# A retention layer and two expert layers on one core: the second expert layer begun on two turned tiles, and turns of the first put in front of a loop

## The chip, the core and the metric

The kernel runs on one core of one Trainium2 chip. The metric is the device time of one execution in microseconds (us). The core's engines are TensorE (PE; PEld is its weight loading), VectorE (DVE), ScalarE (ACT), GpSimd (POOL) and SyncE (SP, which only issues DMAs). Each engine takes its instructions in the order in which the program gives them; engines meet through semaphores.

## The reference

```python
def _attn_ref(q, k, v):                      # 8 batches, 8 heads, 576 positions, 64 dims
    scores = scale * np.matmul(q, k.transpose(0, 1, 3, 2))
    ret = scores * Dmat[None]                # gamma_h ** (i - j) for i >= j, else 0
    return np.matmul(ret, v)

def _moe_ref(x, w_skip, w_gate, w1, w2):     # 4608 tokens of 512, 8 experts, 1024 hidden
    do_compute = x @ w_skip > 0
    xc = x[do_compute]
    e_idx, gate_w = ...                      # largest logit of xc @ w_gate, and its probability
    for e in range(8):
        y[e_idx == e] = gate_w * (relu(xc @ w1[e]) @ w2[e])
    out[do_compute] = xc + y

def _moe2_ref(x, w_gate, w1, w2):
    # (token, expert) pairs in falling order of their logit; each token goes to the first expert
    # that still has room, each expert takes at most 576 tokens
    for e in range(8):
        out[assigned == e] = relu(x[assigned == e] @ w1[e]) @ w2[e]
```

The attention's output is the input of the first expert block, whose output is the input of the second.

## The kernel before, in words

The attention with its gate logits runs first, tile by tile, and ends with a routing step that gives each token of the first block its expert and its place (`route`). Then come the two expert blocks. The program's order is written out by hand: each engine executes in the order in which these Python lines issue instructions.

**An expert in either block.** Its tokens' rows are gathered from DRAM into tiles of up to 128 rows by GpSimd (`gather`, line 619), turned by four transposes on TensorE, copied out by ScalarE as the high part `xTH`, and VectorE subtracts to get the low part `xTL` (`turn`, 634: the products are made in three passes, high with high, high with low, low with high). Weights come as quarters of 512 KB (`w_load`, 229), are split into a high part by ScalarE (`w_split`, 237) and a low one by VectorE (`w_rest`, 251). Layer 1 (`layer1`, 675; `layer1_f`, 652) goes over eight filters of 128 hidden units, 12 matmuls each for a segment of columns; ScalarE and VectorE write the hidden units' high and low parts. Filters 0 and 1 need weight quarter 0, filters 2 and 3 quarter 1, and so on. Layer 2 (`layer2`, 694) multiplies these by w2, and the rows are scattered to DRAM. The first block takes at most 352 tokens of an expert in its regular pass (tiles of 128, 128 and 96); tokens beyond that go through a loop of overflow blocks (`over_blocks`, 897), whose count is computed on the chip (`nov`, 878). In this input it is zero, and the body is not run. The loop's entry and exit stay: every engine loads the count (line 899), and all engines meet before the program goes on. In the kernel before, the loop stands directly behind the issue of the three gathers of expert 0; then come filler matmuls (`warm`, 221, which keep TensorE busy and whose result nobody reads) and the three turns (1051 to 1054). The gates' weights (`gate_parts`, 808; `gate_weights`, 825) are computed in steps within layer 1 of expert 0, as jobs of `slot_a`.

**The second block.** Which tokens an expert takes depends on the experts before it, so the assignment is found in eight phases (`phase`, 1159), one per expert. A phase builds masked logits and claims (1169 to 1176), finds a threshold in five rounds (1180 to 1203; each round is a mask on VectorE, ten small matmuls `cnt`, an intermediate copy `part`, four matmuls `sum`, a comparison `fl`, one matmul `nfl`, and a maximum), gives the expert's number (`eix`, from there on its weights can be loaded), then the list of its tokens (`ids2`, from there on its rows can be gathered), and last updates the state: what room and which tokens are left (1289 to 1319). Phase 0 runs beside the first block's last layer 2, each later phase beside the layers of the expert before it.

Phases and preparations are Python generators. `tick` (1349), called twice in each filter's 12 matmuls and once per filter of layer 2, advances a clock by columns/2400 and lets every task whose time has come issue its next step between the matmuls; the number that a step yields is the time until the next. `LAG` (1165) is added to the waits in which an answer of another engine is expected.

Between the two blocks the order is written out (1376 to 1395): when list 0 is there, two weight quarters are loaded on SyncE's queue and the five tiles gathered, 64 fillers are issued, and then steps of the phases (`go`), weight splits (`sp`), turns and loads on ScalarE's queue alternate as line 1387 lists them. Five `go` are among them: two finish phase 0's state update, three begin the claims of phase 1. Four of the five turns stand in front of layer 1, the fifth is a task of its own. `eil` is a copy of expert 0's number, from which SyncE and ScalarE load the address of its weights. Layer 1 takes two segments, columns 0 to 256 (tiles 0 and 1) and 256 to 576 (tiles 2 to 4), for two filters at a time with expert 0:

```python
1463        hh = layer1(("b", i), [(0, 256), (256, CAP2)], lambda: None, 1 if i else 2, tick, ht=ht)
```

`weights_b` (1411) splits what is left of w1 (`held`, 1409), splits w2, waits for the next expert's number and loads its first quarter; `rows_b` (1445) waits for the next list, gathers its tiles, and turns them once layer 1 is done.

## Time and profile before

| | us |
|---|---|
| median of 3 runs | 971.97 |
| lowest and highest run | 970.97, 974.04 |
| the profiled execution, its own time | 971.05 |
| its span, first to last instruction | 969.3 |
| attention and routing | 0 to about 176 |
| first block, layer 1 of expert 0 to the last layer 2 | 190.4 to 478.9 |
| second block, layer 1 of expert 0 to the end | 493.1 to 969.3 |

The span is what the profile's rows cover; the time around it is 1.75 us. In the rows, times are us from the span's start unless marked ns; a name like `xTL<-trp,xTH` says what is written and what is read; the number in brackets at a row's end is how long the engine stood idle before it, and what ended that. The ends of matmuls are modelled. The granted clock is a share of TensorE's 2.4 GHz: 1.00 or 0.50.

### The profile page before, as it was taken

The numbers are of one execution on the slowest core, as the hardware profiler recorded it, in microseconds if no ns is written. First come the engines' busy times: TensorE is split into PE (matmuls) and PEld (weight loads), VectorE is DVE, ScalarE is ACT, GpSimd is POOL, SyncE is SP. The second block draws the span as 40 slices with busy tenths as digits, with TensorE's granted clock in tenths as the row PEclk, the third lists the DMA queues.
The fourth block names the chain that finished last, engine by engine and source line by source line (L and its number), as shares of the span: only waits on it lengthen the run. The fifth ranks groups of instructions, "written<-read, shape, count | busy, mean of one in ns | idle before, by whom it ended". The sixth has DMA issues, their size and how long they took to land.

```text
span 969.3 us, 20752 instructions
## 1 busy us (share of the span) xinstructions
PE 918.6 (95%) x8356; PEld 768.9 (79%) x8356; DVE 653.6 (67%) x1677; ACT 320.2 (33%) x610; POOL 232.6 (24%) x208
## 2 busy tenths in 40 slices
PE   7899998599999999998969999999999999999997
PEld 7777886498888888886658697887978879797885
DVE  3556576369999999966677767676775767844230
ACT  1233333233434333352042242332423324243330
POOL 2322231203354344231310302104031030320101
PEclk9999999799999999999989999999999999999999
DMA  9999995264454455340160515215061231533201
GB/s 318 356 377 358 347 368 228 79 234 174 159 196 138 160 181 175 133 135 11 40 222 24 205 45 192 80 51 190 34 218 55 101 139 55 207 114 115 87 6 44
DMA packets 57684, 153.96 MB, mean 159 GB/s; under 512 B 8464, under 2 KB 9232, under 8 KB 57328
## 3 DMA queue, kind: packets, MB, share of 16 engines
q1 hardware_dynamic: 40608, 107.50, 31.6%
q0 software_dynamic: 10496, 30.93, 9.1%
q10 hardware_dynamic: 6480, 14.16, 3.9%
q8 instruction: 67, 1.10, 0.5%
q14 instruction: 33, 0.27, 0.1%
HBM read 127.43 MB, written 25.13 MB: 157 GB/s over the span
## 4 chain that ended last, share of the span: by engine, by line
PE 72%; DVE 15%; DMA 7%; issue 3%; ACT 1%; SPq 1%; POOL 1%; POOLq 0%; ACTq 0%; DVEq 0%
PE l1p L660 27%; PE l2p L691 26%; DVE junk L758 5%; PE xTp L445 3%; PE trp L641 3%; PE l2p L714 2%; PE sc L419 2%; DVE w2L L179 2%; DMA vR<-in_v_r_dram 2%; DMA xg<-X,ids 2%; PE xrp L473 1%; DVE xTL L179 1%; DMA kT<-in_k_c_dram 1%; DVE hL L188 1%; PE xTp L442 1%
## 5 line engine op out<-in xcount | busy, mean ns | idle before, releaser
L660 PE MATMUL l1p<-xTH,w1H 128*128 128x320 f32 (+2 forms) x768 | 241.4, 314 | 4.9 <-DVE hL L188 3.0
L660 PE MATMUL l1p<-xTL,w1H 128*128 128x320 f32 (+2 forms) x768 | 234.2, 305 | 2.9 <-DVE xTL L179 2.9
L660 PE MATMUL l1p<-xTH,w1L 128*128 128x320 f32 (+2 forms) x768 | 233.7, 304 | 0.0
L691 PE MATMUL l2p<-w2H,hH 128*128 128x512 f32 (+1 forms) x448 | 187.9, 419 | 0.0
L691 PE MATMUL l2p<-w2H,hL 128*128 128x512 f32 (+1 forms) x448 | 177.2, 396 | 0.0
L691 PE MATMUL l2p<-w2L,hH 128*128 128x512 f32 (+1 forms) x448 | 177.0, 395 | 0.0
L660 PEld LDWEIGHTS l1p<-xTH,w1H 128*128 128x128 f32 x768 | 145.1, 189 | 9.4 <-DVE hL L188 5.6
L660 PEld LDWEIGHTS l1p<-xTL,w1H 128*128 128x128 f32 x768 | 145.1, 189 | 4.2 <-DVE xTL L179 3.8
L660 PEld LDWEIGHTS l1p<-xTH,w1L 128*128 128x128 f32 x768 | 144.9, 189 | 0.0
L188 DVE SCALAR_TENSOR_TENSOR hL<-l1p,hH 128x256 fp32r<-128x256 f32 (+1 forms) x192 | 85.6, 453 | 80.6 <-ACT hH L669 77.1
L720 POOL DMA_INDIRECT out_dram<-y,ids x40 | 41.6, 1040 | 375.9 <-DVE y L179 224.5
L669 ACT ACTIVATE hH<-l1p 128x256 fp32r<-128x256 f32 (+1 forms) x192 | 78.3, 408 | 147.7 <-PE l1p L660 141.1
L691 PEld LDWEIGHTS l2p<-w2H,hH 128*128 128x128 f32 (+1 forms) x448 | 82.9, 185 | 24.7 <-issue 8.3
L758 DVE SCALAR_TENSOR_TENSOR junk<-x,wgb 128x512 f32<-128x512 f32 (+1 forms) x144 | 99.0, 687 | 3.1
L691 PEld LDWEIGHTS l2p<-w2H,hL 128*128 128x128 f32 (+1 forms) x448 | 82.6, 184 | 22.0
L691 PEld LDWEIGHTS l2p<-w2L,hH 128*128 128x128 f32 (+1 forms) x448 | 83.1, 185 | 15.6
L621 POOL DMA_INDIRECT xg<-X,ids x64 | 78.4, 1225 | 55.2 <-issue 25.9
L245 ACT ACTIVATE w1H<-wraw 128x1024 fp32r<-128x1024 f32 x64 | 65.3, 1053 | 41.0 <-DMA wraw<-in_w1b_dram 37.9
L642 ACT ACTIVATE xTH<-trp 128x512 fp32r<-128x512 f32 (+2 forms) x64 | 35.4, 557 | 124.5 <-PE trp L641 113.5
L179 DVE TENSOR_TENSOR w2L<-wraw,w2H 128x1024 fp32r<-128x1024 f32 x60 | 72.7, 1214 | 0.0
L245 ACT ACTIVATE w2H<-wraw 128x1024 fp32r<-128x1024 f32 x64 | 67.4, 1055 | 15.4 <-PE l2p L691 7.3
L179 DVE TENSOR_TENSOR w1L<-wraw,w1H 128x1024 fp32r<-128x1024 f32 x60 | 71.5, 1216 | 0.4
(258 smaller groups left out, 1136.6 us busy)
## 6 DMA issues: line engine op xcount, KB each, us to landing
wraw<-in_w2a_dram SPq DMA_DIRECT2D x31, 512.0 KB
wraw<-in_w1b_dram SPq DMA_DIRECT2D x30, 512.0 KB
wraw<-in_w2b_dram SPq DMA_DIRECT2D x30, 512.0 KB
wraw<-in_w1a_dram SPq DMA_DIRECT2D x28, 512.0 KB
kT<-in_k_c_dram SPq DMA_DIRECT2D x36, 256.0 KB
qT<-in_q_c_dram SPq DMA_DIRECT2D x36, 256.0 KB
vR<-in_v_r_dram SPq DMA_DIRECT2D x36, 256.0 KB
X<-xo ACTq DMA_DIRECT2D x36, 256.0 KB
```

Of the source, the lines that this page charges most:

```text
L179: V.tensor_tensor(o, x, y, op)
L188: V.scalar_tensor_tensor(o, x, sc, y, op0, op1)
L245: nc.scalar.activation(h, r, AF.Copy)
L445: nc.tensor.matmul(xTp[o, hh, x:x + P], lhsT=d["vs"][:, 2 * pr + hh, :], rhs=d["ret"][:, hh, pr, :], start=(c == 0), stop=True, skip_group ...
L621: nc.gpsimd.indirect_dma_start(out=t[0:n, :], out_offset=None, in_=X[:, :], in_offset=bass.IndirectOffsetOnAxis(ap=ids[0:n, :], axis=0))
L641: nc.tensor.transpose(p[:, k, 0:n], g[0:n, k * P:(k + 1) * P], ident[0:n, 0:n])
L642: nc.scalar.activation(h[:, :, off:off + n], p[:, :, 0:n], AF.Copy)
L660: nc.tensor.matmul(o, lhsT=wx[:, c:c + P], rhs=xx[:, k, a:b], start=(n == 0), stop=(n == 11))
L669: nc.scalar.activation(hh[0][:, f, a:b], o, AF.Relu)
L691: nc.tensor.matmul(p[0:n, :], lhsT=x[:, f, off:off + n], rhs=y[:, c:c + 512], start=(f == 0 and j == 0), stop=(f == 7 and j == 2))
L720: nc.gpsimd.indirect_dma_start(out=dst[:, :], out_offset=bass.IndirectOffsetOnAxis(ap=idx, axis=0), in_=src[0:n, :], in_offset=None)
L758: V.scalar_tensor_tensor(j[0:n], x2[0:n], 1.0, wgb[e // 4][0:n, e % 4], ALU.mult, ALU.mult, accum_out=dst[0:n, e:e + 1])
```

## The change

In front of the first block, the gate parts are computed ahead, the first two tiles are turned, then comes the overflow loop, two of the three gate multiplications, and the third turn; the fillers there are dropped. Within the loop, tiles get other places in memory. In the second block, the gathers are issued first; the first step of the state update (which now includes the copy `eil`) comes ahead of SyncE's two weight loads, the second ahead of the fillers, of which 48 are left. Two tiles are turned and two weight quarters split; then layer 1 begins, four filters at a time. The three other turns and the remainder of quarter 1 are steps of a task, `entry`; the phases go on 3.5 clock units later, the splits of quarters 2 and 3 after 5. ScalarE's queue issues its loads behind the second split instead of between the turns, and the last w2 quarter waits in `held`. The lag is 0.25 instead of 0.4 in phase 1, and 0.9 instead of 1.0 from phase 2 on.

```diff
@@ -632,7 +632,10 @@
     xT = {}
 
     def turn(key, i, n, off, spare=False):
-        if i == 0:
+        if key == "o":
+            xo = xp.tile([P, 2, 4, P], F32R, name="xTo", tag="hL")
+            xT[key] = (xo[:, 0], xo[:, 1])
+        elif i == 0:
             xT[key] = (xp.tile([P, 4, CAP2], F32R, name="xTH", tag="xTH"), xp.tile([P, 4, CAP2], F32R, name="xTL", tag="xTL"))
         h, l = xT[key]
         g = xg[key, i]
@@ -806,7 +809,6 @@
 
 
     def gate_parts():
-        gs.clear()
         ex = rt("c1", [P, NC, E])[:, 0:NT]
         tt(ex, LG[:, :, 0:8], last(m1, E), ALU.subtract)
         nc.scalar.activation(ex, ex, AF.Exp)
@@ -820,12 +822,10 @@
             V.tensor_copy(gj, gw)
             tt(gw, gw, gj, ALU.subtract)
             gs.append(gj)
-            yield
 
     def gate_weights():
-        for j, _ in enumerate(gate_parts()):
-            if j:
-                tt(MV[:, :, 24 + 24 * j:48 + 24 * j], OHhi, pairs(gs[j - 1], 24), ALU.mult)
+        for j in range(3):
+            tt(MV[:, :, 48 + 24 * j:72 + 24 * j], OHhi, pairs(gs[j], 24), ALU.mult)
             yield
         gp = psm.tile([P, 72], F32, name="gp", tag="sm")
         for t in range(NT):
@@ -898,18 +898,15 @@
         kept = dict(wt)
         with tc.For_i(0, nc.values_load(nov[0:1, 0:1], min_val=0, max_val=NT + E), 1):
             over_lists()
-            for _ in gate_parts():
-                pass
             om = rt("om", [P, NT])
             ts(om, ohi, blk, ALU.is_equal)
-            MO = xp.tile([P, NT, 6], BF16, name="MO", tag="hL")
+            MO = xp.tile([P, NT, P + 6], BF16, name="MO", tag="hH")
             for j, c in enumerate((u_t, v_t, gs[0], gs[1], gs[2], oex)):
-                tt(MO[:, :, j], om, c, ALU.mult)
-            OHo = xp.tile([P, NT, P], BF16, name="OHo", tag="hH")
-            tt(OHo, mid(iota, NT), last(olo, P), ALU.is_equal)
+                tt(MO[:, :, P + j], om, c, ALU.mult)
+            tt(MO[:, :, 0:P], mid(iota, NT), last(olo, P), ALU.is_equal)
             p = psm.tile([P, 6], F32, name="ovp", tag="sm")
             for t in range(NT):
-                nc.tensor.matmul(p, lhsT=OHo[:, t, :], rhs=MO[:, t, :], start=(t == 0), stop=(t == NT - 1))
+                nc.tensor.matmul(p, lhsT=MO[:, t, 0:P], rhs=MO[:, t, P:P + 6], start=(t == 0), stop=(t == NT - 1))
             ov6 = rt("ov6", [P, 6])
             V.tensor_copy(ov6, p)
             oxi = rt("oxi", [P, 1], I32)
@@ -1046,12 +1043,17 @@
 
 
     over()
-    over_blocks()
+    gps = gate_parts()
+    next(gps)
+    next(gps, None)
     gws = gate_weights()
     t0 = turns(0, T1, (2,))
-    for n, j in enumerate(t0):
-        warm(ps1, "l1", 16 if n == 0 else 4)
-        j()
+    t0[0]()
+    t0[1]()
+    over_blocks()
+    next(gws)
+    next(gws)
+    t0[2]()
     for j in gathers_a(1):
         j()
     pend = []
@@ -1091,7 +1093,7 @@
         ga, (la1, la2) = gathers_a(e + 1), loads_a(e + 1)
         if e == 0:
             sta = state()
-            jobs += [j for n in range(4) for j in (lambda: next(gws, None), la1[n])] + [lambda: next(gws, None)]
+            jobs += [la1[0], lambda: next(gws), la1[1], lambda: next(gws, None)] + la1[2:4]
         else:
             jobs = jobs[0:2] + [ga[0]] + jobs[2:4] + [ga[1]] + jobs[4:5] + [ga[2]] + la1
         hh = layer1(e, [(0, CAP1)], slot_a)
@@ -1162,7 +1164,7 @@
         sb = rt("sb", [P, 2, NC], BF16)
         mc = rt("mc", [P, 1])
         es = rt("es", [P, E])
-        LAG = (0.3, 0.4, 1.0)[min(i, 2)]
+        LAG = (0.3, 0.25, 0.9)[min(i, 2)]
         MASK = 1.6
         if i < E - 1:
             if i:
@@ -1282,8 +1284,6 @@
                                  start=(q == 0), stop=(q == 3), tile_position=(0, 32 * a), skip_group_check=True)
         iv = rt("iv", [P, 5])
         ts(iv, p[:, 5:10], -1.0, ALU.add)
-        if i == 0:
-            V.tensor_copy(eil, eix[:, 0:1])
         stt(ids2[:, i, :], p[:, 0:5], 64.0, iv, ALU.mult, ALU.add)
         yield "list"
         if i < E - 1:
@@ -1295,6 +1295,8 @@
             ts(cnd, inv0, 1.0 / ZMUL, ALU.mult)
             V.reciprocal(cnd, cnd)
             ts(zu, zu, cnd, ALU.mult, lo0, ALU.add)
+            if i == 0:
+                V.tensor_copy(eil, eix[:, 0:1])
             X2 = rt("X2", [P, NC, E], BF16)
             tt(X2, OH[:, 0:NC], last(gh, E), ALU.mult)
             cc = rt("cc", [P, E])
@@ -1376,23 +1378,35 @@
     tasks.remove(t)
     while 0 not in listed:
         next(gen)
+    for j in gathers_b(0):
+        j()
+    go = lambda: next(gen)
+    go()
     lb = load_b(0)
-    sp = halves("w1", swap=True)
-    for j in lb[0][0:2] + gathers_b(0):
+    lb[0][0]()
+    lb[0][1]()
+    go()
+    warm(ps1, "l1", 48)
+    t0 = turns(("b", 0), T2, (2, 3))
+    t0[0]()
+    w_split("w1", 0, "later", swap=True)
+    w_rest("w1", 0)
+    t0[1]()
+    w_split("w1", 1, "later", swap=True)
+    la = load_b(0, nc.scalar)
+    for j in la[0][2:4] + la[1][0:1]:
         j()
-    t0 = turns(("b", 0), T2, (2, 3))
-    warm(ps1, "l1", 64)
-    go = lambda: next(gen)
-    la = load_b(0, nc.scalar)
-    for j in [go, go, sp[0], t0[0], sp[1], go, t0[1], go] + la[0][2:4] + [t0[2], go, t0[3], la[1][0], la[1][1]] + sp[2:5] + lb[1][2:4]:
-        j()
-
-    def last_turn():
-        t0[4]()
-        yield 0
-
-    task(last_turn())
-    task(gen)
+
+    def entry():
+        w_rest("w1", 1)
+        for j in t0[2:5]:
+            yield 0.7
+            j()
+        for j in la[1][1:3]:
+            j()
+
+    task(entry())
+    task(gen)[1] = clock[0] + 3.5
 
     def post_b(i):
         def post(j, n, p):
@@ -1406,10 +1420,12 @@
     lay = [0]
     done = set()
 
-    held = []
+    held = [lb[1][3]]
 
     def weights_b(i):
         if held:
+            if i == 0:
+                yield 5.0
             for c in (2, 3):
                 w_split("w1", c, "later", swap=True)
                 yield 1.2
@@ -1460,7 +1476,7 @@
     for i in range(E):
         mine = [task(weights_b(i)), task(rows_b(i))]
         ht = xp.tile([P, 8, 64], F32, name="hT", tag="junk", bufs=1)
-        hh = layer1(("b", i), [(0, 256), (256, CAP2)], lambda: None, 1 if i else 2, tick, ht=ht)
+        hh = layer1(("b", i), [(0, 256), (256, CAP2)], lambda: None, 1 if i else 4, tick, ht=ht)
         lay[0] += 1
         whole = [wt["whole", "w2", c] for c in range(4)]
         layer2_half(ht, whole, post_b(i), 4, tick)
```

## Rows read from the trace of the kernel before

**Rows 1.** TensorE's waits, 481 to 530 us: in total, times, longest.

```profile
PE trp L641 <- DMA xg<-X,ids: 3.9, 1, 3.9
PE l1p L660 <- DVE xTL L179: 2.4, 2, 1.4
...
PE cnt L1191 <- DVE M L179: 0.9, 1, 0.9
```

**Rows 2.** TensorE's waits, 530 us to the last layer.

```profile
PE idp L1272 <- DVE OHl L179: 1.8, 3, 0.9
```

**Rows 3.** Layer-1 matmuls by stretch: us, PE, PEld, clock, DMA.

```profile
493.06:530.02 36.96, 31.23 (x192) 27.55 (x192) 0.95 0.28 99
562.72:590.45 27.73, 27.41 (x192) 25.62 (x192) 1.00 0.13 48
911.43:936.88 25.45, 25.44 (x192) 25.17 (x191) 1.00 0.09 32
```

**Rows 4.** Chain of waits at the overflow loop: start us, us, what.

```profile
177.47 0.97 POOL xg L621
...
178.74 4.65 DMA xg<-X,ids
183.39 1.58 issue
...
190.98 1.07 PE l1p L660 x5
```

**Rows 5.** Line 899 on VectorE's sequencer: ns min/median/max, first and last start.

```profile
L899 DVEq EVENT_SEMAPHORE  x13: 21/50/3641, 179.1 to 184.4; - x13
...
L899 DVEq TENSOR_LOAD <-nov x1: 662/662/662, 178.2 to 178.2; - x1
```

**Rows 6.** Chain of waits, 482 to 504 us.

```profile
483.57 5.88 DMA xg<-X,ids
...
489.49 1.14 PE trp L641 x4
...
490.65 0.61 ACT xTH L642
...
491.97 1.13 DVE w1L L179
...
493.78 0.60 DVE xTL L179
```

**Rows 7.** VectorE by line, 196 to 205 us: busy us, mean ns.

```profile
L179 DVE TENSOR_TENSOR MV<-OHhi,gw 128x864 bf16<-128x864 bf16 x3 | 1.8, 601 | 0.0
```

**Rows 8.** Stretches at the low clock: us, five engines, clock, DMA.

```profile
179.16:189.40 10.24, 4.42 (x34) 4.31 (x35) 0.69 (x1) 0.96 (x2) 3.35 (x4) 0.50 0.39 113
...
503.43:506.84 3.41, 3.41 (x19) 3.19 (x16) 2.28 (x6) 1.44 (x3) 0.00 (x0) 0.50 0.04 18
```

**Rows 9.** DMA queues, 484.5 to 487 us: packets, MB, share.

```profile
q1 hardware_dynamic: 241, 0.92, 96.1%
```

**Rows 10.** VectorE in order of time: start us, us.

```profile
487.86 0.16 DVE L179 TENSOR_TENSOR rem<-rem,cct 128x8 f32<-128x8 f32 x1 [3.31 <-remote]
...
497.30 3.48 DVE L179 TENSOR_TENSOR w1L<-wraw,w1H 128x1024 fp32r<-128x1024 f32 x3
...
539.74 0.16 DVE L188 SCALAR_TENSOR_TENSOR ids<-idq,iv 128x5 int32<-128x5 f32 x1
```

**Rows 11.** TensorE in order of time.

```profile
481.80 3.75 PE L224 MATMUL idle<-ones 128*128 128x128 bf16 x64
...
494.43 0.38 PE L660 MATMUL l1p<-xTL,w1H 128*128 128x256 f32 x1 [0.95 <-DVE xTL L179]
...
556.74 0.46 PE L641 MATMUL trp<-cs,xg 64*128 64x64 f32 x4
```

**Rows 12.** ScalarE in order of time.

```profile
491.14 1.05 ACT L245 ACTIVATE w1H<-wraw 128x1024 fp32r<-128x1024 f32 x1
```

**Rows 13.** VectorE's busy time, 491.28 us to the layer's end.

```profile
491.28:530.02 38.74, 31.47 (x85) 0.93 0.28 96
```

## The prediction, made before the changed kernel ran

> **What bounds the kernel now.** I began with the clock line and the waits of TensorE, to find where the engine that carries the kernel stands still. From 530 us to the end it waits 1.8 us for VectorE [rows 2]; an edit behind that point has little to win. Between 481 and 530 us it stands 3.9 us for the first gathered tile of the second block, 2.4 us for the low parts of the turned tiles and 0.9 us for a mask of the claims [rows 1]. The table of the layer-1 matmuls shows the same from another side [rows 3]: the same 192 matmuls take 36.96 us for the second block's first expert, 27.73 us for its second, and 25.45 us for the last, which has no claims beside it. So some 9 us are lost in that layer. The other serial place is the loop over overflow blocks in front of the first block, whose body does not run here. Its chain [rows 4] goes from the gathers to the last landing at 183.39, then 1.58 us of restart; layer 1 flows from 190.98. The loop makes every engine wait until gathers still under way have landed.
>
> **Part 1: turns and gate parts in front of the loop.** The second gather is issued at 177.47; with the 4.65 us that the third took [rows 4] it lands at 182.1. Four transposes cost 1.14 us at the low clock, the copy 0.61, the low part 0.60 [rows 6]: TensorE is done at 183.3, ScalarE at 183.9, VectorE at 184.5. VectorE loaded the loop's count at 178.2 and had waited 3.64 us when the barrier opened [rows 5], so it reached it at 183.39 - 3.64 = 179.75, 1.55 us after the load. That load now follows the second tile's low part: begun between 183.9 and 184.5, the barrier opens at 185.5 to 186.1, no longer held by the third gather (183.39). With 1.58 us of restart TensorE is back at 187.3. The third tile has 96 rows of 128: three quarters of 1.14 and 0.61 give 188.6 and its low part, about 0.5, 189.1. The two gate multiplications now in front of that low part, 0.60 us each [rows 7], run from 187.3 to 188.5, beside the transposes and the copy; without this cover they would cost 1.2 us. The rest of the gate parts runs while VectorE waits for the gathers. **Gain 190.98 - 189.1 = 1.9 us.** Moving the gates' 36 small matmuls from the end of layer 1 into its middle changes no amount of work, and the gathers of expert 1, about 2 us later, are wanted only in layer 2: nothing.
>
> Against it stands the clock. It was at 1.2 GHz, half, from 179.16 to 189.40 [rows 8]; 24 filler matmuls and three turns ran from 184.97 on, and layer 1 began at 2.4 GHz. The fillers are gone, and TensorE does two short turns, stands some 4 us and then starts on real work, so the low stretch probably lasts into layer 1. Another low stretch lasted 3.41 us [rows 8]; at half speed it costs half, 1.7 us. Bounds 0 and 1.7; I take 1.2, nearer to the upper, as less work than before precedes the layer. Part 1 nets **0.7 us** (0.2 to 1.9). "TensorE: Matmul & The Clock Gate" of the Trainium skill (Part 1, the HAM clock gate) says the throttled state is the default and activity releases it, which speaks against taking fillers out; the row agrees.
>
> **Part 2: when layer 1 of the second block starts.** Now the first gather goes out at 483.57 and lands 5.88 us later; its turn starts at 489.49 [rows 6]. The third gather of part 1 needed 4.65 us [rows 4]. The difference is the weight loads: from 484.5 to 487 us all 241 packets are theirs, on SyncE's queue, and none are the gather's [rows 9]. The change copies the expert's number six short VectorE instructions later and so issues the loads behind the gather. Landing between 488.2 (483.57 + 4.65) and 489.4; I take 488.7, since the loads still come before the later gathers. The small product of the state update, which now precedes the fillers, costs TensorE nothing measurable; before, VectorE waited 3.31 us behind 64 of them, until 487.86 [rows 10], although their own rows end after 3.75 us [rows 11]. So 48 fillers take between 2.8 us (3.75 x 48/64) and 4.5 us (487.86 - 481.80, for 64, in proportion), from 484.55 (487.86 - 3.31, when VectorE had its operand ready): done at 487.4 to 489.1, inside the same bounds. The rest of the state update, 487.86 to 491 before, then runs inside the gather's wait.
>
> From its turn to the first steady matmul took 494.43 - 489.49 = 4.94 us [rows 6, 11]. Out goes the third step of the claims between a weight remainder and the second tile's low part (491.97 + 1.13 = 493.10 to 493.78, 0.68 us [rows 6]). In comes the split of the first weight quarter, 1.05 us on ScalarE [rows 12], which now stands behind the first tile's copy (before it ran while the gather was awaited); its remainder starts after 0.61 + 1.05 instead of 0.61 + 0.69: 0.4 us. So layer 1 flows from 488.7 + 4.94 - 0.68 + 0.4 = **493.4** (492.9 to 494.2) against 494.43.
>
> "DMA: Bandwidth & Descriptors" of the Trainium skill (Queues, rings and completion order) says each DMA engine serves its queues in turn, packet by packet. By that rule the gather would have shared the engines from the start, which rows 9 do not show, and moving the loads would win nothing.
>
> **Part 3: length of that layer.** The matmuls alone take 25.45 us; five rounds of claims add 27.73 - 25.45 = 2.3 [rows 3]; three turns now stand inside the layer, each half of 1.14 at the full clock, 1.7 together. The waits behind late low parts [rows 1] go: four filters over two tiles' 256 columns come first, and the third to fifth turn have over 5 us.
>
> What is late next is VectorE. It has 31.47 us of work from 491.28 to the end of the layer [rows 13], and every answer of a claims round queues behind whatever stands ahead: a weight remainder is 3.48/3 = 1.16 us [rows 10]. The later start (3.5 units of 2,400 columns) puts the first mask at the tenth tick, beside the remainder of quarter 2, and the shorter lag (0.25 for 0.4) asks for each answer after about one tick, 0.64 or 0.8 units. Laid out tick by tick, with each engine in order, TensorE waits 0.4 us for the first mask, 0.85 for its sum, 0.15 in the second round, 0.7 in the third and 0.3 in the last: 2.4 us. Bounds: 0 (before, one wait of 0.9 us for a mask was all that the claims cost it [rows 1]) and five remainders, 5.8. Clock: the layer begins after broken work, as before at 503.43, so 0 to 1.7 again; I take 1.0. The layer ends at 493.4 + 25.45 + 2.3 + 1.7 + 2.4 + 1.0 = 526.25 instead of 530.02. **Gain 3.8 us** (from 492.9 + 29.25 = 522.1, 7.9 better, to 494.2 + 29.45 + 5.8 + 1.7 = 531.2, 1.1 worse).
>
> Behind it I count nothing: layer 2 keeps its waits for the list's one-hots (1.8 [rows 2], could go or grow by as much), the lag of 0.9 instead of 1.0 has as little cover to lose, and the quarters 2 and 3 and the fourth w2 quarter are issued later but have the layer's first half. The overflow loop's new tiles are not reached.
>
> **The rivals.** *Loads and gathers share:* part 2 wins nothing (494.2), the rest holds: 967.6. *VectorE keeps up:* no waits in part 3, clock high at once: 971.05 - 7.9 - 0.7 = 962.5; for it speaks that the same rounds cost one wait of 0.9 us before, against it that the same work of VectorE now has some 5 us less. *Nothing comes of it:* the early start is not one, since the first turn and the split queue on ScalarE, both low stretches last 1.7 us and waits reach 4.5: part 1 gives 0.2, the layer ends at 494.2 + 29.45 + 4.5 + 1.7 = 529.85: 970.7. *Slower:* the list of expert 1 comes late. It stood at 539.74 [rows 10], 9.7 us behind the layer; its fifth turn ended at 557.2 [rows 11], 5.5 us ahead of the next layer at 562.72 [rows 3]. Those 5.5 us are the point: if rounds that start later and queue behind remainders push the list further than that behind the layer's end, each further us is paid in full. With the layer 1.1 us worse, as at its upper bound, and 2.5 us paid: 974.7 in the profile, 975.6 on the runs' scale.
>
> **How the numbers follow.** 971.05 - 0.7 - 3.8 = 966.55 for the profiled execution, which lies 0.9 below the median of 971.97; I give **967.0**, between that and 967.5. A difference below 0.3% (2.9 us) cannot be told from none. Chances: forecast 0.47, sharing 0.13, keeping up 0.12 (these three faster: 0.70, as a 0.02 of the forecast's tail falls short), nothing 0.23, slower 0.05. The range, 963.2 to 970.8, takes in the first, second and most of the fourth, and leaves out the best end and the slower case.
>
> **What would show it.** Right: the barrier opens near 186 us; a low clock reaches into layer 1 of the first block; the first turn of the second block starts before 489; three turns lie among the first four filters; first steady layer 1 under 34 us, with small waits for VectorE's masks and sums. Wrong: the first turn at 489.5 or later (loads not the cause), a first layer above 35 us (VectorE's queue), or a wait of TensorE for gathered tiles ahead of the next layer (the list).

## The result: slower, and where the profile after shows it

The changed kernel takes **979.54 us** (median of 8 runs, 976.56 to 982.49) against 973.1 us of the kernel before in the same comparison: ratio **1.0071 [1.0048, 1.0095]**. Forecast were 967.0 us and a gain. The profiled execution after took 979.02 us, its span is 977.2 us (before 971.05 and 969.3).

Up to the second block's second expert the changed kernel is ahead, though less by the change than the absolute times suggest. TensorE's rows at the start of the second block, after (start us, us, what; idle before it and what ended that):

```profile
488.91 0.95 PE L644 MATMUL trp<-cs,xg 128*128 128x128 f32 x4
490.65 0.66 PE L644 MATMUL trp<-cs,xg 128*128 128x128 f32 x4 [0.79 <-DMA xg<-X,ids]
492.23 0.39 PE L663 MATMUL l1p<-xTH,w1H 128*128 128x256 f32 x1 [0.92 <-ACT xTH L645]
493.61 0.58 PE L663 MATMUL l1p<-xTL,w1H 128*128 128x256 f32 x1 [0.99 <-DVE xTL L179]
```

The first turn no longer waits for its gather, and steady work starts at 493.61 (494.43 in [rows 11]). But this execution was 0.8 us ahead before any changed line: the last matmul into `qc`, a product of the routing, stands at

```profile
170.35 0.21 PE L319 MATMUL qc<-OHe,ones 128*128 128x80 bf16 x1 [0.90 <-DVE base L185]
```
```profile
169.54 0.21 PE L319 MATMUL qc<-OHe,ones 128*128 128x80 bf16 x1 [0.91 <-DVE base L185]
```

before and after. From there to the end of the first block both executions take 308.5 us, and from that end to steady layer 1 both take 15.5 us. So the 0.8 us are not the change's. The gather did come sooner (first packet 1.7 us after its issue, 3.6 before); yet the fillers behind it now ran at the low clock, 48 of them in 5.28 us where 64 had taken 3.75 [rows 11], and TensorE left them for the first turn only at 488.91:

```profile
483.84 5.28 PE L224 MATMUL idle<-ones 128*128 128x128 bf16 x48
```

The layer-1 matmuls of the second block's first, second and last expert, after, by stretch (us, PE, PEld, clock, DMA), answer to [rows 3]:

```profile
492.23:527.12 34.89, 30.64 (x192) 27.06 (x192) 0.95 0.26 92
558.51:586.76 28.25, 27.73 (x192) 25.70 (x191) 1.00 0.14 48
919.23:944.77 25.54, 25.54 (x192) 25.27 (x191) 1.00 0.09 32
```

The first is 2.1 us shorter, and the second starts at 558.51 instead of 562.72: **4.2 us ahead**. Of these, 0.8 us are the earlier start above, 2.1 us the shorter layer, and 1.3 us lie behind it: there two waits for `OHl` cost 1.5 us before (536 to 538 us), and TensorE waits for nothing after (527.2 to 558.5). By the end the kernel is 7.9 us behind, so 12.1 us go in a stretch for which the prediction had nothing. TensorE's waits from 530 us on, after, answer to [rows 2], where `OHl` stands with three waits; the only other wait there was 0.4 us for a gathered tile:

```profile
PE trp L644 <- DMA xg<-X,ids: 5.1, 3, 2.0
PE l1p L663 <- DVE hL L188: 0.8, 1, 0.8
PE idp L1274 <- DVE OHl L179: 0.8, 1, 0.8
PE cnt L1193 <- DVE M L179: 0.7, 2, 0.4
```

TensorE now stands for gathered tiles far behind the block's start. One such place, around the list of expert 3: VectorE's list, GpSimd's gathers, SyncE's weight loads (`x3` groups three issues), and TensorE's wait.

```profile
650.31 0.17 DVE L188 SCALAR_TENSOR_TENSOR ids<-idq,iv 128x5 int32<-128x5 f32 x1
```
```profile
651.25 1.31 POOL L621 DMA_INDIRECT xg<-X,ids  x1 [30.76 <-PE l2p L717]
...
657.86 0.92 POOL L621 DMA_INDIRECT xg<-X,ids  x1 [0.30 <-issue]
```
```profile
647.52 2.32 SPq L234 DMA_DIRECT2D wraw<-in_w1b_dram  x3
651.05 8.92 SPq L234 DMA_DIRECT2D wraw<-in_w2b_dram  x3
```
```profile
658.98 0.66 PE L644 MATMUL trp<-cs,xg 128*128 128x128 f32 x4 [2.04 <-DMA xg<-X,ids]
```

The gathers go out among the loads. In the kernel before, the loads of this expert began at 651.15 and the first gather followed 6 us behind:

```profile
651.15 1.59 SPq L234 DMA_DIRECT2D wraw<-in_w1b_dram  x3
```
```profile
657.37 1.32 POOL L621 DMA_INDIRECT xg<-X,ids  x1 [1.58 <-issue]
```

The DMA queues after, from 651.5 to 655 us (packets, MB, share):

```profile
q1 hardware_dynamic: 301, 1.08, 89.3%
```

All packets but one are of the weights' queue; of the gather issued at 651.25 none moves in these 3.5 us, as in [rows 9]. What holds them back the traces do not say. Once packets of both queues move, they share the engines, as before from 657.5 to 661 us:

```profile
q1 hardware_dynamic: 276, 0.97, 69.6%
q0 software_dynamic: 109, 0.35, 26.6%
```

The turn, however, is placed by the planner's clock and comes whether or not the tile has landed. Right behind this wait TensorE drops to the low clock once more (three low stretches after: us, five engines, clock, DMA; the first answers to [rows 8], the second covers the fillers):

```profile
179.01:192.66 13.65, 8.47 (x29) 7.01 (x30) 4.98 (x14) 2.15 (x4) 3.21 (x3) 0.50 0.38 127
482.80:489.62 6.82, 5.83 (x53) 5.78 (x53) 3.24 (x17) 0.00 (x0) 4.74 (x5) 0.50 0.74 255
660.29:663.70 3.41, 3.41 (x12) 2.72 (x11) 3.23 (x8) 0.47 (x1) 1.22 (x1) 0.50 0.73 256
```

What moved the list? Reading each list's time against the end of its block's layer 1 gives the theory. The lists of experts 1 to 6 come behind the end of the layer before by (us; each the start of `ids` less the last layer-1 matmul):

| kernel | 1 | 2 | 3 | 4 | 5 | 6 |
|---|---|---|---|---|---|---|
| before | 9.7 | 7.3 | 7.3 | 7.7 | 7.2 | 7.2 |
| after | 11.3 | 7.5 | 4.2 | 0.5 | -3.1 | -5.7 |

Before, a phase lasts as long as a pair of layers and the list keeps its place. After, it walks forward by some 3.5 us per expert; this is called the drift below. The lag is not only a cover for single answers: 19 yields of a phase carry it (three in each of five rounds and four more), so 0.9 instead of 1.0 makes the phase 1.9 planner units shorter.

The drift is already in the program. A step is issued at the first tick at or after its time, ticks lie 0.64 to 0.85 units apart, and the next time counts from at most 0.4 units before that tick. Worked through with these rules and the yields of the two kernels, the lists of experts 2 to 6 stand 5.33 units behind the layer, each of them, before, and 5.33, 2.56, 0.0, -2.88 and -5.12 units after. The plain sum of a phase's yields does not show this: it is 42.7 units with the lag of 1.0 and 40.8 with 0.9, against 46.9 that a pair of layers ticks. With 1.0 the whole difference goes into waiting for ticks.

### The profile page after: what moved, and what is told of

It is laid out like the page before. It is cut to its first block, busy times and chain, and to the rows that moved or that the text cites. A ratio compares the mean times of both kernels' runs of the same rounds, so it can differ in the third digit from the quotient of the medians.

```text
span 977.2 us, 20671 instructions
## 1 busy us (share of the span) xinstructions
PE 923.8 (95%) x8316; PEld 769.5 (79%) x8316; DVE 652.0 (67%) x1677; ACT 319.3 (33%) x610; POOL 226.3 (23%) x208
## 4 chain that ended last, share of the span: by engine, by line
PE 56%; DVE 18%; issue 3%; DMA 2%; ACT 1%; another core or an unknown queue 0%; POOLq 0%; ACTq 0%; DVEq 0%
PE l2p L694 24%; PE l1p L663 23%; DVE junk L761 5%; DVE w2L L179 3%; PE l2p L717 3%; PE trp L644 2%; DVE hL L188 2%; DVE w1L L179 2%; DMA xg<-X,ids 1%; DVE xTL L179 1%; DVE x L188 1%; PE cnt L1193 1%; PE idp L1274 1%; DVE M L179 1%; PE idle L224 1%
## 5 line engine op out<-in xcount | busy, mean ns | idle before, releaser
L663 PEld LDWEIGHTS l1p<-xTH,w1H 128*128 128x128 f32 x768 | 145.7, 190 | 10.5 <-DVE hL L188 6.4
L621 POOL DMA_INDIRECT xg<-X,ids x64 | 74.2, 1160 | 163.5 <-PE l1p L663 51.4
L723 POOL DMA_INDIRECT out_dram<-y,ids x40 | 38.7, 967 | 284.9 <-ACT y L1414 121.7
L179 DVE TENSOR_TENSOR ret<-sc,cs 128x512 f32<-128x512 f32 x72 | 46.3, 685 | 33.5 <-PE sc L419 33.5
```

Of the source, the lines that this page charges most:

```text
L179: V.tensor_tensor(o, x, y, op)
L621: nc.gpsimd.indirect_dma_start(out=t[0:n, :], out_offset=None, in_=X[:, :], in_offset=bass.IndirectOffsetOnAxis(ap=ids[0:n, :], axis=0))
L663: nc.tensor.matmul(o, lhsT=wx[:, c:c + P], rhs=xx[:, k, a:b], start=(n == 0), stop=(n == 11))
L723: nc.gpsimd.indirect_dma_start(out=dst[:, :], out_offset=bass.IndirectOffsetOnAxis(ap=idx, axis=0), in_=src[0:n, :], in_offset=None)
```

## The experiments

Every run stands beside the kernel before on the same chip. From each profiled execution I also took three stretches: A from the first matmul into `qc` (line 319) to the end of the first block, B to the start of layer 1 of the second block's second expert, C to the last matmul's end. A also holds some 32 us of routing that no edit touches and that differs by up to 2 us from one execution to the next.

| kernel | median us | ratio to before | A | B | C |
|---|---|---|---|---|---|
| before | 971.2 to 973.1 | 1 | 340.8 | 83.8 | 400.3 |
| after | 979.54 | 1.0071 [1.0048, 1.0095] | 341.4 | 80.4 | 412.4 |
| after_lag10 | 970.91 | 0.9991 [0.9965, 1.0017] | 340.3 | 80.1 | 405.4 |
| before_lag09 | 978.50 | 1.0068 [1.0037, 1.0098] | 341.9 | 85.0 | 409.1 |
| before_part1 | 974.07 | 1.0029 [1.0005, 1.0053] | 341.2 | 85.2 | 401.9 |
| after_no_part1 | 979.12 | 1.0066 [1.0033, 1.0098] | 339.9 | 80.4 | 410.4 |
| lag09_once | 971.66 | 0.9995 [0.9966, 1.0023] | 341.5 | 80.7 | 403.5 |
| lag09_pad | 970.18 | 0.9960 [0.9938, 0.9981] | 342.0 | 82.0 | 401.1 |
| lag09_hold | 974.69 | 1.0010 [0.9987, 1.0034] | 340.2 | 81.7 | 406.7 |
| lag09_once_no_part1 | 971.35 | 0.9983 [0.9960, 1.0006] | 339.1 | 82.0 | 404.6 |
| lag10_drift | 980.16 | 1.0084 [1.0057, 1.0111] | 341.2 | 80.1 | 414.3 |
| before_lag09_pad | 975.38 | 1.0044 [1.0011, 1.0077] | 338.8 | 82.2 | 404.9 |
| pad_again | 969.84 | 0.9982 [0.9955, 1.0009] | 341.3 | 80.3 | 401.7 |
| pad_no_part1 | 967.98 | 0.9962 [0.9936, 0.9988] | 339.7 | 80.2 | 400.9 |
| pad_fill84 | 974.10 | 1.0033 [1.0007, 1.0058] | 343.8 | 82.0 | 401.3 |
| pad_fill20 | 971.19 | 0.9987 [0.9957, 1.0016] | 339.8 | 80.5 | 403.8 |
| best_again | 970.74 | 0.9984 [0.9951, 1.0018] | 339.5 | 81.8 | 400.6 |

**The lag, in both kernels.**

```diff
-        LAG = (0.3, 0.25, 0.9)[min(i, 2)]
+        LAG = (0.3, 0.25, 1.0)[min(i, 2)]
```

> The changed kernel with one number put back: the lag of phases 2 and later is 1.0 again, not 0.9. Theory (the lag): the shorter lag brings the lists forward against the layers, so that gathers queue among the weight loads and the turned tiles come late; that is where the 12 us behind the second block's first layer went. Then this kernel keeps the 4 to 5 us gained ahead of that layer and loses nothing behind it: 967 to 970 us, the stretch from layer 1 of the second expert to the end at 406 to 409 us, list 3 some 7 us behind the layer's end and not 4. Rival (the offset): the lists' place is set by the start of the phases 3.5 later and by phase 1's lag of 0.25, and the lag behind them matters little: 977 to 981 us, waits for gathered tiles near 659 and 776 as in the changed kernel.

And in the kernel before:

```diff
-        LAG = (0.3, 0.4, 1.0)[min(i, 2)]
+        LAG = (0.3, 0.4, 0.9)[min(i, 2)]
```

> The kernel before with the lag of phases 2 and later at 0.9 and nothing else. Theory (the lag): the lists come earlier here too and collide with the weight loads: 976 to 986 us, with TensorE waiting for gathered tiles behind 560 us. Rival (the offset): without the shifted start the shorter lag only moves small operations about: 971 to 975 us. Second rival (the sum of both): a loss of less than half of the changed kernel's 12 us, 974 to 978 us, as the lists begin from a later place than in the changed kernel.

Measured: 970.91 and 978.50. The one number brings the changed kernel 8.6 us back (7.8 by the ratios) and costs the kernel before 7 us; the rival by the offset falls in both. But 970.91 misses the theory's 967 to 970. Stretch C is 405.4 and not 400.3. The lists now hold their place, but at 10.2 to 11.9 us behind the layer, 3 us later than before. TensorE's waits from 560 us on in after_lag10 show what this place costs:

```profile
PE idp L1274 <- DVE OHl L179: 4.0, 5, 1.0
```

Once per phase the product over the list's one-hots is asked for before VectorE has written them; between 560 us and the end the kernel before has one such wait, of 0.3 us. With the lists drifting in before_lag09 the gathered tiles are late again:

```profile
PE trp L641 <- DMA xg<-X,ids: 4.1, 4, 1.8
PE idp L1272 <- DVE OHl L179: 2.4, 4, 1.0
```

**The two halves of the change.** before_part1 is the kernel before with the first block's hunks of the diff (lines 632 to 1093), after_no_part1 has all the others.

> The kernel before with the first block's half of the change alone: the first tiles turned and two of the gate's parts made in front of the loop, the loop's matrices in one tile. The second block is as before. Theory (the trace of the changed kernel: all layers of the first block 1.0 us earlier): 971.5 to 973 us, ratio 0.998 to 1.000. Rival (this part has a share of the loss, by what it does to the lists of the second block): above 975 us.

> The changed kernel without the first block's half: turns and gate parts stay in the loop's wake, the second block is as changed. Theory (all of the loss is of the second block): 979.5 to 981.5 us, about 1 us over the changed kernel, with the waits for gathered tiles behind 640 us. Rival (the two halves meet): at or under 976 us.

Measured: 974.07, where 971.5 to 973 was expected, and 979.12, just under the 979.5 to 981.5 expected. The loss belongs to the second block. The first half, however, does not gain.

**Drift or cover?** A shorter lag does two things: it shortens the phase, and it leaves VectorE less time ahead of each small matmul. Two kernels keep the short lag and take the drift away, by one short phase only (lag09_once) or by a longer last yield (lag09_pad):

```diff
-        LAG = (0.3, 0.25, 0.9)[min(i, 2)]
+        LAG = (0.3, 0.25, 0.9, 1.0)[min(i, 3)]
```

> The changed kernel with the lag of 0.9 in phase 2 alone and 1.0 from phase 3 on. Theory (place and drift): 0.9 makes a phase some 2.7 us shorter than a pair of layers, so that each list comes about 3.5 us earlier against its layer than the one before it (11.3, 7.5, 4.2, 0.5, -3.1, -5.7 us behind the end of layer 1), while 1.0 holds the place; with 1.0 throughout the lists stand 10.3 us behind the layer and each phase's matmuls with the list's digits wait 0.6 to 1.1 us for VectorE (4.0 us in all), at the 7.2 us of the kernel before they do not. So with one short phase the lists stand near 7.5 us throughout: 965.5 to 968.5 us, no wait of TensorE behind 560 us over 1 us in total. Rival (the lag itself: a shorter lag is a shorter cover wherever it stands): as with 1.0 throughout less one phase's change, 970 to 973 us. Rival (the gain ahead of the second expert cannot be kept): 970 to 972 us with 406 us turned into 410 us behind layer 1 of the second expert by waits that are new.

```diff
             tt(asg, asg, t2, ALU.add)
-            yield 1.5
+            yield 3.4 if i > 1 else 1.5
```

> The changed kernel, lag 0.9 kept in all phases from 2 on, and the last yield of those phases longer by 1.9 (19 lags of 0.1 less in each), so that a phase has its old length. Theory (drift): the lists stand 7 to 8 us behind the layer's end throughout and the loss goes: 965.5 to 969 us, no wait for gathered tiles behind 560 us. Rival (cover: 0.1 us less between VectorE's work and the small matmuls that read it is what costs): the drift is gone but each phase still waits: 975 to 980 us, with TensorE waiting for VectorE's tiles in every phase.

One makes the opposite: the long lag with a phase as short as the changed kernel's.

```diff
-        LAG = (0.3, 0.25, 0.9)[min(i, 2)]
+        LAG = (0.3, 0.25, 1.0)[min(i, 2)]
...
-            yield 2.0 + LAG
+            yield (1.3 if i > 1 else 2.0) + LAG
...
-            yield 1.5
+            yield 0.3 if i > 1 else 1.5
```

> The changed kernel with the lag at 1.0 from phase 2 on, but those phases shortened elsewhere by the same 1.9 us: 0.7 off the yield ahead of the counts' matmul and 1.2 off the last yield. Every other matmul of a phase has its old lag; the phase is as short as with 0.9. Theory (drift): the lists run forward against the layers as in the changed kernel (7, 4, 0.5, -3 us behind layer 1's end), TensorE waits for gathered tiles: 976 to 981 us. Rival (the lag of 0.9 itself costs by lost cover): no more than the run with 1.0 and nothing shortened, 970 to 973 us.

| kernel | list 1 | 2 | 3 | 4 | 5 | 6 |
|---|---|---|---|---|---|---|
| after_lag10 | 11.3 | 10.5 | 10.3 | 11.9 | 10.2 | 10.3 |
| lag09_once | 11.3 | 7.3 | 7.3 | 7.3 | 6.4 | 7.3 |
| lag09_pad | 11.3 | 7.3 | 7.3 | 7.3 | 6.4 | 7.3 |
| lag10_drift | 11.3 | 10.4 | 7.2 | 4.2 | -0.8 | -4.1 |
| before_lag09 | 10.9 | 6.6 | 3.1 | -0.8 | -4.0 | -6.4 |

Measured: lag09_pad 970.18, lag10_drift 980.16. With the short lag everywhere and no drift the loss is gone, though 970.18 lies 1.2 us above the range expected (the rival by lost cover had 975 to 980); with the long lag and the drift it is there in full. TensorE's waits from 560 us on, lag09_pad and then lag10_drift:

```profile
PE trp L644 <- DMA xg<-X,ids: 0.6, 1, 0.6
PE trp L644 <- issue: 0.5, 2, 0.3
```
```profile
PE trp L644 <- DMA xg<-X,ids: 6.0, 3, 3.0
PE idp L1274 <- DVE OHl L179: 2.2, 4, 1.0
PE pfx L1234 <- DVE sb L1230: 1.4, 1, 1.4
PE cnt L1193 <- DVE M L179: 1.4, 2, 1.0
```

This settles it for the changed kernel: the drift costs, not the cover. lag09_once has the same places; its 971.66 is above the 965.5 to 968.5 expected, though C is 403.5, 1.9 us under after_lag10. What it has over lag09_pad (some 1.5 us, with gathered tiles and masks waited for 2.6 us in all) was not told apart.

The same pad in the kernel before:

> The kernel before with the lag of 0.9 and the last yield of phases 2 and later longer by 1.9, so that a phase keeps its length. With 0.9 alone this kernel lost 1.0068 [1.0037, 1.0098]. Theory (drift): that loss goes, 970.5 to 973.5 us, ratio within 0.998 to 1.002. Rival (the lag itself): 976 to 980 us.

Measured 975.38, 1.0044 [1.0011, 1.0077], a miss: 3 of the 7 us come back, not all, and as this interval overlaps that of before_lag09, even these 3 are not clear of chance. Its lists hold at 6.2 us behind the layer, and TensorE waits three times for gathered tiles behind 590 us, 2.9 us in all (in a profiled execution of 969.61 us, a fast one of this kernel). So in that kernel the short lag, or a list one us earlier, may still cost; this stays open.

**How much of the drift is the gathers?** The lists drift on, but the gathers are held to their old place.

```diff
+    lend = [0.0]
...
-        while i + 1 not in listed:
+        while i + 1 not in listed or lay[0] < 2 * i + 1 or clock[0] < lend[0] + 6.2:
             yield 0
...
         lay[0] += 1
+        lend[0] = clock[0]
```

> The changed kernel, lag 0.9 and its drift kept, but the gathers of the next expert held until 6.2 of the planner's microseconds behind the end of layer 1 (where the kernel before has them), however early the list. Theory (collision): the waits for gathered tiles near 659 and 776 us and the low clock behind the first of them go (about 5 us of waits and 1.7 us of clock); what the drifting phases cost by meeting VectorE elsewhere stays: 971 to 975 us. Rival (the drift costs by VectorE, not by the gathers): 977 to 981 us. Rival (all by the gathers): 967 to 970 us.

Measured 974.69: 4.9 us of the 979.54 go (5.9 by the ratios). The waits for gathered tiles are down to 0.4 us, and no low clock is left between the first layer and the kernel's last 3 us. What remains is VectorE (TensorE's waits from 560 us on, lag09_hold):

```profile
PE cnt L1193 <- DVE M L179: 2.0, 3, 0.9
PE idp L1274 <- DVE OHl L179: 0.8, 1, 0.8
PE l1p L663 <- DVE hL L188: 0.8, 1, 0.8
PE pfx L1234 <- DVE sb L1230: 0.7, 1, 0.7
```

So of some 9 us that the drift costs (979.54 less 969.84 to 970.91), about 5 go with gathers behind weight loads. For most of the rest the rows above stand, 4.3 us of waits, nearly all of the phases' small matmuls for VectorE; that the drift brings these about by meeting a layer's own work there was not tried by itself.

**The first half, again, and the best version.** Two pairs compare a repaired kernel with and without the first block's half: lag09_once with lag09_once_no_part1, and the padded kernel (pad_again is lag09_pad once more) with pad_no_part1.

> The second block's half alone, with the lag of 0.9 in phase 2 alone and 1.0 from phase 3 on; the first block is as before. Beside the same with the first block's half it prices that half. Theory (the layers of the first block came 1.0 us earlier in the changed kernel's trace): 966.5 to 969.5 us, 0.5 to 1 us over the kernel with both halves. Rival (the first block's half loses, as the run of it alone, 1.0029 [1.0005, 1.0053], has it): 963 to 966 us, 2 to 3 us under the kernel with both.

> The changed kernel with the phases' length put back by the last yield (0.9 kept), as run once (0.996 [0.9938, 0.9981]); here beside the same without the first block's half. Theory: the gain ahead of the second expert's layer 1, 3 to 4 us, is kept: ratio 0.995 to 0.998. Rival (the first figure was chance): 0.998 to 1.001.

> The same with the first block as before: the second block's half alone, phases at their old length. Rival to my forecast of 0.7 us for the first block's half, by the runs so far (1.0029 [1.0005, 1.0053] alone; no difference in two pairs of kernels with and without it): the half is worth nothing or costs, so this kernel is at the same time or up to 2.5 us faster, ratio 0.993 to 0.997. Theory of the forecast: 0.7 us slower than with it, ratio 0.996 to 0.999.

Measured 971.35, above both ranges; 969.84, by its ratio at the edge of its rival's range; and 967.98, 1.9 us under the same with the half, where the forecast's side had 0.7 us over and the rival's up to 2.5 us under. By ratios the half makes +0.0029 (alone), +0.0005 (changed kernel), +0.0012 (one short phase) and +0.0020 (padded) in four pairs. Each but the first is within chance, and the padded kernels of other comparisons (0.9960 with it, 0.9984 without) go the other way; the forecast gain of 0.7 us shows nowhere for sure, a loss above 2 us neither.

The traces are sharper, if one counts from the last matmul into `qc`, behind which the first gather is issued 5.7 us later in every trace. (The 50.9 and 53.0 us of an expectation below count from the first such matmul, though it says the last, and so take in the routing.) The second matmul of layer 1 starts 18.1 us later with the half (mean of eight traces) and 20.5 without (seven): 2.4 us ahead. But layer 2 of that expert starts at 36.9 against 37.1, only 0.2 us ahead and within the traces' spread of 0.4, and the first block ends at 308.3 against 307.5. This last loss has one place: from the start of that layer 2 to the block's end it takes 271.3 to 271.6 us in every trace that has a low stretch near 452 us, and 270.0 to 270.1 in those without. All eight traces with the half have this stretch, and two of the seven without; whether the half sets it was not tried.

The chain at the loop after says where the start comes from, as [rows 4] before (start us, us, what), and line 899 on VectorE's sequencer as [rows 5]:

```profile
185.12 0.92 PE trp L644 x4
...
186.32 1.13 DVE MV L179 x2
187.45 0.48 DVE xTL L179
...
187.97 4.18 PE l1p L663 x13
```
```profile
L899 DVEq EVENT_SEMAPHORE  x13: 21/50/50, 184.7 to 186.0; - x13
...
L899 DVEq TENSOR_LOAD <-nov x1: 543/543/543, 183.5 to 183.5; - x1
```

VectorE, the last to come, goes through its semaphores at the barrier from 184.7 to 186.0; TensorE is let go earlier, as its third turn at 185.12 shows. Steady layer 1 begins at 187.97 at half clock, which lasts to 192.66. Low clock there takes 13.65 us in six of the eight traces with the half and 10.24 in two; without it 6.83 in five of seven and 10.24 in two. Does it last because the fillers are gone? They were put back in the padded kernel, all three lines in pad_fill84 and the last one alone in pad_fill20; best_again is pad_no_part1 once more:

```diff
+    warm(ps1, "l1", 44)
     t0[0]()
+    warm(ps1, "l1", 20)
     t0[1]()
+    warm(ps1, "l1", 20)
     over_blocks()
```

> The changed kernel with the phases' length put back, both halves in, and fillers on TensorE where it waits ahead of and beside the loop's start: 44 before the first turn, 20 behind it, 20 behind the second. In the traces so far the first block's half brings the second steady matmul of layer 1 of the first expert 2.0 us forward against the last counting matmul in front of it (50.9 against 53.0 us behind it, means of eight and six traces), but low clock lasts 10.2 to 13.7 us there and not 6.8 to 10.2, and the layer ends 1.4 us later against that matmul. Theory (it removed the fillers, so TensorE idles more and the clock comes back later): with fillers low clock there is at most 6.8 us and this kernel is 2 to 3 us under the same without them: 966 to 968 us, at or under the one without the first block's half. Rival (the low clock there is set by the time of the loop and its barrier, fillers ahead of it change nothing): 969 to 971 us, low clock as before. Second rival (fillers that run at the low clock push the turns back): over 971 us.

> The same with only the 20 fillers behind the second turn, in the 2.3 us that TensorE waits for the loop. Theory (fillers ahead of the layer bring the clock back): part of the gain, low clock 6.8 to 10.2 us, 967.5 to 969.5 us. Rival (nothing): 969 to 971 us, low clock 10.2 to 13.7 us.

> The second block's half alone with the phases' length put back, as run once (0.9962 [0.9936, 0.9988]), beside the two with the first block's half and fillers. Theory: 0.994 to 0.998 again, 966.5 to 969.5 us. Rival (the first figure was chance): 0.998 to 1.000.

Measured 974.10, 971.19 and 970.74. 84 fillers shorten the low stretch but move it: it starts at 190.14, just ahead of layer 1 at 192.05 (low stretch in pad_fill84), while TensorE waits longer ahead of its third turn, 5.2 us instead of 2.3:

```profile
190.14:196.97 6.83, 5.82 (x20) 5.22 (x21) 0.76 (x2) 0.95 (x2) 0.85 (x1) 0.50 0.47 144
```
```profile
PE trp L644 <- DMA xg<-X,ids: 5.2, 1, 5.2
```

With 20 there is low clock for 6.83 and again for 3.41 us, and no gain. The second rival of pad_fill84 holds, and the rival of pad_fill20: no such filling wins the half back. Why the clock stays low longer there is not settled beyond that.

**The version to keep** is the second block's half with the phases' length put back: 967.98 and 970.74 in two comparisons, 0.9962 [0.9936, 0.9988] and 0.9984 [0.9951, 1.0018]. It is about 9 to 12 us under the changed kernel, and 1.5 to 4 us under the kernel before, a lead that one of the two intervals alone tells from none: best_again, at 0.9984, came out on the side of its rival (0.998 to 1.000), by which part of the first figure was chance.

## Why the prediction was wrong, point by point

**Part 1, start of layer 1.** Right in its mechanism: 1.9 us forecast, 2.2 in the trace after and 2.4 in the means, counted from the last matmul into `qc`. VectorE comes last, after a load of the count (183.5) that had moved behind the low part, as worked out. Put on the time scale of the trace before (0.8 us later), the other engines are let go at 185.5, forecast 185.5 to 186.1. TensorE is back 1.4 us sooner than the 187.3 forecast, which gains nothing, since the multiplications and the low part on VectorE come after it.

**Part 1, the clock.** Mis-sized. I took 1.2 us with an upper bound of 1.7, half of one stretch of 3.41. In the trace after, 4.69 us of low clock lie behind the first steady matmul (187.97 to 192.66), 2.3 at half speed. That takes the 2.2 us back, so layer 2 starts no sooner than before (37.2 us behind the last matmul into `qc` in both; 0.2 sooner in the means) instead of 0.7. The layer itself takes 20.26 us (186.60 to 206.86) instead of 16.06, but its end does not compare: the gates' 36 matmuls, which stood between the layers before (206.29 to 207.50), are now inside it. The rule of the Trainium skill weighed there ("TensorE: Matmul & The Clock Gate", Part 1) spoke against taking the fillers out, and the longer low stretch agrees with it, though fillers put back ahead of the loop won nothing.

**Part 2.** Right by luck in its number, 493.61 for a forecast 493.4: the 0.8 us that it is earlier than before are the earlier start of this execution. Counted from the end of the first block, steady layer 1 starts after 15.5 us in both traces, and after 15.4 (thirteen) and 15.5 (four) in the means: nothing of the 1.0 us came. The gather's part holds: issued ahead of the loads it moves its first packet after 1.7 us instead of 3.6. The chain behind the first turn holds as well, 4.7 us for 4.66 forecast. What failed is the term of the fillers: I scaled rows at the full clock to at most 4.5 us for 48, and at the low clock they took 5.28 and held the first turn to 10.85 us behind the block's end, where the gather had held it to 10.60. By the round-robin of the Trainium skill's "DMA: Bandwidth & Descriptors" (Queues, rings and completion order) the gather would have had packets between 651.5 and 655 if its queue had work by then; the trace shows none, and not why.

**Part 3.** Right in kind: counted from the end of the first block the layer ends 2.1 us earlier, forecast 3.8, within the bounds. (Their lower end uses 29.25 where the same terms make 29.45, 0.2 us.) It takes 33.5 us from the first steady matmul, where I had said under 34 and added up 32.85; the small waits for masks and sums are there (next lines, TensorE's waits from 500 to 527 us after), 1.5 us where I had laid out 2.4.

```profile
PE sum L1199 <- DVE part L1195: 0.8, 3, 0.4
PE cnt L1193 <- DVE M L179: 0.7, 1, 0.7
```

Over all traces, B is 80.9 us with the second half (thirteen) and 84.1 without (four), a gain of 3.1 us; in the pair before and after it is 3.4, of which 1.3 come behind the layer, from waits for the list's one-hots that I had left as they were.

**The step that failed:** "Behind it I count nothing: ... the lag of 0.9 instead of 1.0 has as little cover to lose". It looked at one answer at a time and asked whether 0.1 us of cover would be missed there. It did not add up the 19 yields of a phase nor compare a phase's length, ticks included, with a pair of layers, which the kernel's lines allow: that the lists stood 7.2 to 7.7 us behind the layer, expert after expert, was a balance. In its place the runs show some 9 us of loss by drift, of which holding the gathers returns 5. My slower rival had the list coming late; it came early, and its cost was the place of the gathers in the DMA queues. I had a sign for it in "what would show it" (waits for gathered tiles), but with the wrong cause, and a chance of 0.05.

## What to carry to other kernels

Where side work is interleaved with the main engine's by a planner, the length of a round is a period: compare it with the main loop's period before changing any delay. Step through the planner's own rule for this, with its rounding to ticks, since the plain sum of the delays (42.7 units here, for a loop of 46.9) does not give it; and look in the trace at the side work's place in each turn, not only in the first. A list that comes earlier is not better if its gathers then meet bulk loads that are already queued. Put the length back with one yield at the round's end if shorter single delays are wanted.

## What was not expected of the hardware

A gather waited behind queued weight loads without a packet for 3.5 us and more (after, 651.5 to 655 us, far from the block's start), as one had for 2.5 us before [rows 9]. And removing idle time in front of a layer is not all gain: with steady work 2.4 us earlier, layer 2 began only 0.2 us earlier, as low clock (13.65 or 10.24 us of it, against 10.24 or 6.83) reached into layer 1. Fillers that meet the low clock are themselves a delay: 48 took 5.28 us, where 64 had taken 3.75. Another low stretch, of 3.41 us near 452 us, stands in all eight traces with the first block's half (fillers aside) and in two of seven without it, and is worth 1.4 us of the block's length; what sets it was not tried. Runs of one and the same kernel lie up to 16 us apart (before, 965.4 to 981.2 over all comparisons), so no single profiled execution ranks kernels 3 us apart.
